# Rows scattered by half batches, the first weights spread over eight blocks, the first tiles' plan and gathers earlier, and a GpSimd drain behind the third-last tile

## The chip, the cores and the metric

One core of one Trainium2 chip. The metric is device microseconds of one execution. A run has a span, from the first to the last instruction of its record, and in every run here the time is the span plus 1.7 to 1.8 us.

A run also has a granted TensorE clock (1 is full speed) and a state, fast or slow. The state is relative to the other runs of the same kernel in the same session. That matters here: the kernel before took about 520.5 us at clock 0.99 on some chips and about 558 us at clock 0.96 on others, and both are called fast. No chip was met in both conditions, so chip and hour can't be told apart. I call the first chips undisturbed and the second disturbed, by nothing but the time of the kernel before in the same session. Runs are only compared within one session.

## The reference

Windowed attention with 8 memory keys per head, then routed experts. Sizes: 4 batches of 768 tokens, 8 heads of 64, so 512 channels; 8 experts with 1024 hidden channels; all float32.

```python
for c in range(S // 32):                       # 32 queries see 16 before, 8 after, 8 memory keys
    a = softmax(scale * q_c @ concat(mem_k, k_ctx).T)
    out[:, :, chunk] = a @ concat(mem_v, v_ctx)
x = out.transpose(0, 2, 1, 3).reshape(B, S, 512)
for b in range(B):
    prev_e = -1
    for s in range(S):
        fresh_e = argmax(logits[b, s])         # x @ w_gate
        e = fresh_e if s == 0 or local_gate[b, s] < 0.5 else prev_e
        prev_e = e
        h = relu(x[b, s] @ w1[e])
        y[b, s] = softmax(logits[b, s])[e] * (h @ w2[e])
```

## The kernel before

Attention goes in 32 blocks of 96 tokens, 8 to a batch. Routing runs beside it: logits for four blocks, the chosen expert of each token, its rank among that expert's tokens. When a whole batch is ranked, its token rows are scattered by GpSimd into a list in DRAM that is sorted by expert. The expert phase then takes tiles of 128 rows from that list. The first five tiles (the early ones) are planned from the first two batches alone, so that they can start while the other two are still being routed.

```python
def route_rows(r, b, x):                            # one whole batch
    r_ps = xps.tile([QB, NQB, E], F32, name="r_ps", tag="xps")
    for n in range(NQB):                            # NQB = 8
        nc.tensor.transpose(r_ps[:, n], rank[:, QB * n:QB * n + QB], identity=ident[:E, :E])
    # ... VectorE: rows and probabilities
    for n in range(NQB):                            # eight scatters in a row
        ins = nc.gpsimd.indirect_dma_start(out=x_dram[:, :], out_offset=..., in_=x[0:QB, n], ...)

# when what is done, in blocks
        plan_at(after, n + 3, lambda b=b, half=half: route_ranks(routes[b], b, half))
        if half:
            plan_at(after, n + 3, lambda b=b: route_places(routes[b]))
            plan_at(after, n + 4, rows, b)
    n = NQB * FORE + HALF + 5
    plan_at(after, n, plan_begun)
    plan_at(after, n + 1, planned)
    plan_at(after, NB - 5, early_gathered)          # gathers of the five early tiles
    for n in range(NB - 6, NB):
        plan_at(after, n, some_pieces, 1 if n < NB - 4 else FULL)   # weights of tiles 0 and 1
    # ... attention blocks
        if n == NB - 1:
            first_turned()                          # tile 0's rows transposed
    # ... expert phase
    for i in range(SURE):                           # 24 tiles
        ht = hidden(xt, w1_sb, between.get(i, {}))
        # ... transposes of the next tile
        stored = product(ht, w2_sb, tile_xs[i], past)   # ends with the tile's scatter
```

The order of TensorE's matmuls is fixed by the program in the attention phase and in tile 0, so one matmul that waits holds up all behind it. `xps` is a ring of two PSUM buffers that all transposes of the attention phase share.

## Time and profile before

| | time, us | granted clock |
|---|---|---|
| the run that the profile shows | 520.58 | 0.993 |
| timed runs | 559.29, 557.59, 573.73 | not listed |

The profile's own run is 39 us shorter than the median of the timed ones. One line of the page of the kernel before, beside those that the prediction shows: the granted clock in 40 slices of the span in tenths.

```profile
PEclk9999999999999999999999999999999999999997
```

No slice but the last is below nine tenths of full speed, and the profiled run itself took 520.58 us. So either the timed runs met another condition, or their 39 us more lie outside the span.

### The profile page before, as it was taken

How to read it: one execution, taken by the hardware profiler on the slowest of the kernel's cores; microseconds unless marked ns; L12 is line 12 of the kernel's file. 1: busy time of each engine (PE TensorE's matmuls, PEld its weight loads, DVE VectorE, ACT ScalarE, POOL GpSimd, SP SyncE). 2: the span in 40 equal slices, each digit the busy share in tenths (PEclk: the TensorE clock that was granted, in tenths of full speed). 3: DMA queues.
4: the chain of work that ended last, by engine and by line, in shares of the span. 5: the costliest groups of instructions: out<-in, count | busy, mean ns of one | idle time of the engine just before them, and what ended most of it. 6: DMA issues, size and time to landing. Idle time of an engine off the chain costs nothing. (4 is left out here: it accounts for less than half of the span.)

```text
span 518.9 us, 9415 instructions
## 1 busy us (share of the span) xinstructions
PE 503.4 (97%) x3606; PEld 384.5 (74%) x3606; DVE 98.0 (19%) x362; ACT 113.2 (22%) x234; POOL 96.8 (19%) x141
## 2 busy tenths in 40 slices
PE   8999999999999999999999999999999999999991
PEld 5999898876777777777777777777777777677770
DVE  1456667663330000000000000000001000000000
ACT  4555555521111111010111101111011101011110
POOL 2000323444343111001112222111211000100000
PEclk9999999999999999999999999999999999999997
DMA  9987797599999999999898899999998881299200
GB/s 301 368 258 233 199 348 224 197 392 360 406 343 390 416 415 412 419 397 354 312 330 324 327 336 358 342 340 351 358 320 327 295 317 51 87 405 415 112 21 18
DMA packets 52760, 157.97 MB, mean 304 GB/s; under 512 B 7708, under 2 KB 11806, under 8 KB 52705
## 3 DMA queue, kind: packets, MB, share of 16 engines
q1 hardware_dynamic: 44352, 135.40, 71.2%
q0 software_dynamic: 6720, 20.78, 10.8%
q10 hardware_dynamic: 1632, 1.08, 0.7%
q8 instruction: 32, 0.52, 0.4%
q14 instruction: 24, 0.19, 0.1%
HBM read 144.62 MB, written 13.40 MB: 305 GB/s over the span
## 5 line engine op out<-in xcount | busy, mean ns | idle before, releaser
L754 PE MATMUL y_ps<-w_sb,ht 128*128 128x512 f32 x416 | 183.0, 592 | 0.0
L743 PEld LDWEIGHTS h_ps<-gxt,w_sb 128*128 128x128 f32 x1408 | 160.7, 192 | 10.1 <-issue 10.0
L743 PE MATMUL h_ps<-gxt,w_sb 128*128 128x128 f32 x1408 | 161.1, 275 | 0.0
L754 PEld LDWEIGHTS y_ps<-w_sb,ht 128*128 128x128 f32 x416 | 76.9, 190 | 86.6 <-issue 85.4
L759 POOL DMA_INDIRECT out_dram<-y,to x27 | 27.2, 1006 | 228.6 <-ACT y L758 195.2
L680 DVE COPY gxt<-g_ps 128x512 f32<-128x512 f32 x22 | 15.2, 691 | 273.5 <-PE g_ps L677 273.4
L746 ACT ACTIVATE ht<-h_ps 128x512 f32<-128x512 f32 x54 | 32.3, 597 | 154.4 <-PE h_ps L743 153.0
L758 ACT ACTIVATE y<-y_ps,xs 128x512 f32<-128x512 f32 x24 | 16.5, 687 | 162.6 <-PE y_ps L754 149.8
L613 PE MATMUL o_ps<-vt,pt 128*96 128x65 f32 x512 | 49.3, 249 | 0.1
L613 PEld LDWEIGHTS o_ps<-vt,pt 128*96 128x96 f32 x512 | 46.1, 165 | 2.3 <-issue 0.6
L461 POOL DMA_INDIRECT x_dram<-x,row x32 | 30.5, 953 | 73.8 <-DVE fresh L404 63.6
L613 PEld LDWEIGHTS s_ps<-qt,kt 64*128 64x128 f32 x512 | 29.9, 188 | 6.2 <-issue 2.6
L613 PE MATMUL s_ps<-qt,kt 64*128 64x96 f32 x512 | 32.7, 277 | 0.5 <-ACT pt L344 0.4
L743 PE MATMUL h_ps<-held_xt,w_sb 128*128 128x128 f32 x256 | 29.3, 275 | 0.9 <-ACTq _compat.py:109 0.9
L743 PEld LDWEIGHTS h_ps<-held_xt,w_sb 128*128 128x128 f32 x256 | 28.9, 192 | 1.7 <-ACTq _compat.py:109 1.7
L344 ACT ACTIVATE pt<-s_ps,mask_mid 128x256 f32<-128x256 f32 x72 | 28.2, 481 | 5.8 <-PE s_ps L613 5.7
L354 DVE TENSOR_TENSOR x<-o_ps,rinvs 96x256 f32<-96x256 f32 x64 | 26.1, 417 | 1.5 <-DMA x_dram<-x,row 0.3
L362 ACT COPY xt<-xt_ps 128x384 f32<-128x384 f32 x32 | 15.3, 479 | 34.2 <-PE xt_ps L613 34.2
L572 POOL DMA_INDIRECT xs<-x_dram,rows_late x19 | 18.3, 961 | 13.2 <-DMA x_dram<-x,row 7.7
L353 DVE RECIPROCAL rinvs<-o_ps 96x4 f32<-96x4 f32 x64 | 10.5, 171 | 36.0 <-PE o_ps L613 34.2
L756 POOL TENSOR_TENSOR to<-xs,past_late 128x1 int32<-128x1 int32 x19 | 3.5, 185 | 69.2 <-DMA out_dram<-y,to 64.7
L613 PE MATMUL xt_ps<-ident,x 96*128 96x96 f32 x128 | 16.0, 247 | 0.0
(162 smaller groups left out, 209.3 us busy)
## 6 DMA issues: line engine op xcount, KB each, us to landing
w_sb<-in_w_dram SPq DMA_DIRECT2D x216, 512.0 KB, 8.1
kt<-in_k_dram SPq DMA_DIRECT2D x32, 256.0 KB, 4.5
vt<-in_v_dram SPq DMA_DIRECT2D x28, 260.0 KB, 4.4
qt<-in_q_dram SPq DMA_DIRECT2D x32, 192.0 KB, 4.0
vt<-in_v_dram ACTq DMA_DIRECT2D x4, 260.0 KB, 4.8
x_dram<-x,row POOLq DMA_INDIRECT x32, 7.9
out_dram<-y,to POOLq DMA_INDIRECT x27, 6.5
xs<-x_dram,rows_late POOLq DMA_INDIRECT x19, 6.9
```

Source lines behind the costliest of these rows:

```text
L344: nc.scalar.activation(pt[:, :, :, c], st[:, :, :, c], ACT.Exp, bias=m[:, g:g + 1], scale=SCALE)
L354: nc.vector.tensor_tensor(x[:, 0:D].rearrange("p (a u d) -> p u a d", u=2, d=DH)[:, u], o_ps[:, :, 0:DH], rinv.to_broadcast([QB, HP, DH]), ...
L362: nc.scalar.copy(xt, xt_ps)
L461: ins = nc.gpsimd.indirect_dma_start(out=x_dram[:, :], out_offset=bass.IndirectOffsetOnAxis(ap=row[:, n:n + 1], axis=0), in_=x[0:QB, n].bi ...
L572: ins = nc.gpsimd.indirect_dma_start(out=xs.bitcast(I32), out_offset=None, in_=x_dram[:, :], in_offset=bass.IndirectOffsetOnAxis(ap=rows[: ...
L613: return lambda *a, **k: tc.keep_in_program_order(f(*a, **k))
L680: nc.vector.tensor_copy(xt, g_ps)
L743: nc.tensor.matmul(h_ps[:, m], lhsT=w1_sb[:, kk, P * (g + m):P * (g + m) + P], rhs=xt[:, kk], start=(kk == 0), stop=(kk == DK - 1))
L746: nc.scalar.activation(ht[:, g:g + 4], h_ps, ACT.Relu)
L754: nc.tensor.matmul(y_ps, lhsT=ht[:, m], rhs=w2_sb[:, m], start=(m == 0), stop=(m == FK - 1))
L758: nc.scalar.activation(y, y_ps, ACT.Copy, scale=xs[:, D:D + 1])
L759: return nc.gpsimd.indirect_dma_start(out=out, out_offset=bass.IndirectOffsetOnAxis(ap=to, axis=0), in_=y, in_offset=None, bounds_check=NT ...
```

## The change

Five intents. (1) A GpSimd drain behind the third-last tile, so that the last drain finds little left. (The profile lists it on GpSimd's sequencer, as POOLq DRAIN; the last one ended 0.13 us behind the landing of GpSimd's last scatter in the ten profiles with the new drain and 5.35 to 5.84 us behind it in the ten without, as shown below.) (2) A faster start: one warm-up matmul less, q and k first and on two queues. (3) Tile 0's rows transposed two blocks earlier. (4) The plan, the early gathers and the weights of tiles 0 and 1 sooner, these in single pieces over eight blocks. (5) Rows ranked and scattered by half batches, four scatters in a row, so that the gathers can start sooner.

```diff
-WARM = 4
+WARM = 3
-    def load_qk(n):
+    def load_qk(n, queue=nc.sync):
...
+    qks = {n: load_qk(n, nc.scalar) for n in range(2)}
+    qks.update({n: load_qk(n) for n in range(2, LOADS - 2)})
+    vts = {n: load_v(n) for n in range(LOADS - 2)}
...                                              # gate loads from ScalarE's queue to SyncE's
-    def route_rows(r, b, x):
+    def route_rows(r, b, half, x):
-        for n in range(NQB):
+        for n in range(HALF):
             ins = nc.gpsimd.indirect_dma_start(
...
-        if half:
-            plan_at(after, n + 3, lambda b=b: route_places(routes[b]))
-            plan_at(after, n + 4, rows, b)
+        plan_at(after, n + 3, lambda b=b, half=half: route_places(routes[b], half))
+        plan_at(after, n + 4, rows, b, half)
...
-    n = NQB * FORE + HALF + 5
+    n = NQB * FORE + HALF + 2
     plan_at(after, n, plan_begun)
     plan_at(after, n + 1, planned)
-    plan_at(after, NB - 5, early_gathered)
-    for n in range(NB - 6, NB):
-        plan_at(after, n, some_pieces, 1 if n < NB - 4 else FULL)
+    plan_at(after, n + 2, early_gathered)
+    plan_at(after, NB - 3, first_turned)
+    for n in range(NB - 8, NB):
+        plan_at(after, n, some_pieces, 1)
...
         stored = product(ht, w2_sb, tile_xs[i], past)
+        if i == SURE - 3:
+            tc.keep_in_program_order(nc.gpsimd.drain())
```

More of the change, by code (lines that the diff above doesn't have):

```diff
@@ L45 @@
 PAIR = 2
-FULL = 2
 FAR = 4096
-WARM = 4
+WARM = 3
 QUARTER = 32
@@ L262, in load_qk, with load_v @@
         kt = ld.tile([P, HP, P], F32, name="kt")
-        nc.sync.dma_start(kt, k[n])
+        queue.dma_start(kt, k[n])
         return qt, kt
-    def load_v(n, queue):
+    def load_v(n):
         vt = ld.tile([P, H, VW], F32, name="vt")
-        queue.dma_start(vt, v[n])
+        nc.sync.dma_start(vt, v[n])
         return vt
-    qks = {n: load_qk(n) for n in range(LOADS - 2)}
-    vts = {n: load_v(n, nc.scalar) for n in range(LOADS - 2)}
+    qks = {n: load_qk(n, nc.scalar) for n in range(2)}
+    qks.update({n: load_qk(n) for n in range(2, LOADS - 2)})
+    vts = {n: load_v(n) for n in range(LOADS - 2)}
     wg = once.tile([P, DK, QUARTER], F32, name="wg")
     nc.vector.memset(wg, 0.0)
-    nc.scalar.dma_start(wg[:, :, 0:E], w_gate.rearrange("(k p) e -> p k e", p=P))
-    nc.scalar.dma_start(wg[:, :, E:E + 1], w_local.rearrange("(k p) e -> p k e", p=P))
+    nc.sync.dma_start(wg[:, :, 0:E], w_gate.rearrange("(k p) e -> p k e", p=P))
+    nc.sync.dma_start(wg[:, :, E:E + 1], w_local.rearrange("(k p) e -> p k e", p=P))
     fixed = {}
@@ L432, in route_ranks @@
         nc.vector.tensor_tensor_scan(rank[:, of_half], onehot[:, of_half], onehot[:, of_half],
-                                     rank[:, HQ - 1:HQ] if half else base[b], ALU.add, ALU.max)
-        if half:
-            nc.vector.tensor_copy(base[b + 1], rank[:, S - 1:S])
-    def route_places(r):
-        onehot, rank = r["onehot"], r["rank"]
-        for half in range(2):
-            h = slice(HQ * half, HQ * half + HQ)
-            nc.vector.tensor_tensor(rank[:, h], rank[:, h], onehot[:, h], op=ALU.mult)
-        tot = r["tot"] = sm.tile([QB, NQB, 1], F32, name="tot")
-        nc.vector.tensor_reduce(tot, r["ex"], axis=AX.X, op=ALU.add)
+                                     r["edge"] if half else base[b], ALU.add, ALU.max)
@@ new lines, in route_ranks, with route_places @@
+        if half == 0:
+            r["edge"] = sm.tile([E, 1], F32, name="edge")
+        nc.vector.tensor_copy(base[b + 1] if half else r["edge"], rank[:, HQ * half + HQ - 1:HQ * half + HQ])
+    def route_places(r, half):
+        onehot, rank = r["onehot"], r["rank"]
+        h = slice(HQ * half, HQ * half + HQ)
+        nc.vector.tensor_tensor(rank[:, h], rank[:, h], onehot[:, h], op=ALU.mult)
+        tot = r["tot"] = sm.tile([QB, HALF, 1], F32, name="tot")
+        nc.vector.tensor_reduce(tot, r["ex"][:, HALF * half:HALF * half + HALF], axis=AX.X, op=ALU.add)
@@ L445, in route_places @@
         nc.vector.tensor_scalar(tot, tot, 1e-9, None, ALU.add)
         nc.vector.reciprocal(tot, tot)
-    def route_rows(r, b, x):
-        rank, tot, ex = r["rank"], r["tot"], r["ex"]
-        r_ps = xps.tile([QB, NQB, E], F32, name="r_ps", tag="xps")
-        for n in range(NQB):
-            nc.tensor.transpose(r_ps[:, n], rank[:, QB * n:QB * n + QB], identity=ident[:E, :E])
-        row = sm.tile([QB, NQB], I32, name="row", bufs=2)
+    def route_rows(r, b, half, x):
+        j = HALF * half
+        rank, tot, ex = r["rank"], r["tot"], r["ex"][:, j:j + HALF]
+        r_ps = xps.tile([QB, HALF, E], F32, name="r_ps", tag="xps")
+        for n in range(HALF):
+            nc.tensor.transpose(r_ps[:, n], rank[:, QB * (j + n):QB * (j + n) + QB], identity=ident[:E, :E])
+        row = sm.tile([QB, HALF], I32, name="row", bufs=2)
@@ L455, in route_rows @@
         nc.vector.tensor_reduce(row, r_ps, axis=AX.X, op=ALU.max)
         nc.vector.scalar_tensor_tensor(ex, r_ps, 0.0, ex, ALU.is_gt, ALU.mult)
-        prob = sm.tile([QB, NQB, 1], F32, name="prob")
+        prob = sm.tile([QB, HALF, 1], F32, name="prob")
         nc.vector.tensor_reduce(prob, ex, axis=AX.X, op=ALU.add)
-        nc.vector.tensor_tensor(x[0:QB, :, D:D + 1], prob, tot, op=ALU.mult)
-        for n in range(NQB):
+        nc.vector.tensor_tensor(x[0:QB, j:j + HALF, D:D + 1], prob, tot, op=ALU.mult)
@@ L461, in route_rows @@
+        for n in range(HALF):
             ins = nc.gpsimd.indirect_dma_start(
                 out=x_dram[:, :], out_offset=bass.IndirectOffsetOnAxis(ap=row[:, n:n + 1], axis=0),
-                in_=x[0:QB, n].bitcast(I32), in_offset=None).ins
+                in_=x[0:QB, j + n].bitcast(I32), in_offset=None).ins
             tc.declare_no_dep(ins, group="scatters", query=mybir.DependencyQuery.ANY_SYNC, reason="rows are unique")
@@ L634, in half_turned, with rows @@
         logits_turned(lts.pop(g), routes[b]["lt"][:, HALF * half:HALF * half + HALF])
-    def rows(b):
-        route_rows(routes.pop(b), b, xs.pop(b))
+    def rows(b, half):
+        route_rows(routes[b], b, half, xs[b])
     first, after = {}, {}
@@ L652, in everything @@
         plan_at(after, n + 3, lambda b=b, half=half: route_ranks(routes[b], b, half))
-        if half:
-            plan_at(after, n + 3, lambda b=b: route_places(routes[b]))
-            plan_at(after, n + 4, rows, b)
+        plan_at(after, n + 3, lambda b=b, half=half: route_places(routes[b], half))
+        plan_at(after, n + 4, rows, b, half)
     early = {}
@@ L712, in everything @@
         if n + LOADS - 2 < NB:
-            vts[n + LOADS - 2] = load_v(n + LOADS - 2, nc.sync)
-        if n == NB - 1:
-            first_turned()
+            vts[n + LOADS - 2] = load_v(n + LOADS - 2)
         if n > 0:
@@ L779, in everything @@
     left = [f for n in range(NB, NB + HALF + 3) for f in first.pop(n, []) + after.pop(n, [])]
-    TURN, EXPERTS_0, RANKS_0, LOGITS, TURNED, PICKS, EXPERTS_1, RANKS_1, PLACES, ROWS = left
-    between = {0: {1: [TURN], 3: [LOGITS], 4: [EXPERTS_0], 5: [TURNED], 6: [RANKS_0, PICKS]},
-               1: {1: [EXPERTS_1], 2: [RANKS_1, PLACES], 7: [ROWS]}}
+    (TURN, EXPERTS_0, RANKS_0, PLACES_0, LOGITS, ROWS_0, TURNED, PICKS, EXPERTS_1, RANKS_1, PLACES_1,
+     ROWS_1) = left
+    between = {0: {1: [TURN], 3: [LOGITS], 4: [EXPERTS_0], 5: [TURNED], 6: [RANKS_0, PLACES_0, PICKS]},
+               1: {0: [ROWS_0], 1: [EXPERTS_1], 2: [RANKS_1, PLACES_1], 7: [ROWS_1]}}
     late = None
```

## The prediction

> **What bounds the kernel now.** I read the page first, then the idle time of each engine, then the timeline around the joints, last the instructions that each source line left.
>
> ```profile
> span 518.9 us, 9415 instructions
> PE 503.4 (97%) x3606; PEld 384.5 (74%) x3606; DVE 98.0 (19%) x362; ACT 113.2 (22%) x234; POOL 96.8 (19%) x141
> PE   8999999999999999999999999999999999999991
> ```
>
> TensorE is busy for 503.4 of 518.9 us, so 15.5 us is all that a change which only moves work can win, unless it also removes matmuls. Only the first and last of the 40 slices are below nine tenths. So I looked up what the idle 15.5 us are: first the waits of TensorE.
>
> ```profile
> PE z_ps L256 <- DVE xs L253: 1.6, 1, 1.6
> PE h_ps L743 <- ACTq _compat.py:109: 0.9, 1, 0.9
> PE h_ps L613 <- DVE held_xt L680: 0.7, 1, 0.7
> PE s_ps L613 <- ACT pt L344: 0.4, 1, 0.4
> PE s_ps_early L613 <- ACT xt L362: 0.2, 1, 0.2
> ```
>
> That is 3.8 us (columns: total, times, longest), a few gaps of 0.1 us more. The 0.7 us is tile 0's first product waiting for its turned rows, the 0.9 us is the branch for the optional tiles. From tile 3 on the second products start exactly 14.45 us apart but at the branch comparisons, so no weights, gathers or scatters hold TensorE there. The rest, 10.9 us, is the tail: TensorE ends at about 508.0 us. What fills it is in the sequencer's instructions of the kernel's last line:
>
> ```profile
> L856 SPq EVENT_SEMAPHORE  x14: 17/28/27574, 484.7 to 518.8; - x14
> L856 POOLq DRAIN  x3: 40/113/7862, 510.2 to 518.6; - x3
> L759 POOL DMA_INDIRECT out_dram<-y,to x27: 971/1011/1020, 130.6 to 509.5; - x27
> ```
>
> (min/median/max in ns, first and last start in us.) The last row scatter starts at 509.5. SyncE's wait of 27.57 us from 484.7 ends at 512.3: that is its landing. But GpSimd's drain, begun at 510.2, takes 7.86 us, to 518.0, and the closing barrier (0.8 us) stands behind it. So 518.0 - 512.3 = 5.7 us at the end wait for GpSimd's drain alone. The page's chain of waits does not show this, because a drain is a sequencer's instruction and not counted as work.
>
> [...] Here the warm-up passes start 0.85 us apart up to the one at 5.98, then 0.73 and 0.43: warm some 5 us after the first. [...]
>
> **The change, part by part.**
>
> 1. **Drain behind the third-last tile.** The program issues 1 plain and 32 + 27 + 19 + 7 + 5 = 90 indirect DMAs on GpSimd before the end; 7862 ns / 91 = 86 ns each, if the drain goes through all of them. For that reading: the drains with nothing (more) to settle are short (0.19 us at the start, 0.11 and 0.04 us after the long one), so it is no fixed price. The new drain sits where GpSimd is idle: that tile's scatter starts at 481.0, the next at 495.5. 89 x 86 ns = 7.7 us fit into the 14.5. Two scatters remain for the last drain: 0.2 us by the estimate, so it should be done when the last scatter has landed, 512.3. SyncE is ready for the barrier at 513.1 as it is now, and the barrier's 0.75 us follow: end at 513.8 in place of 518.8. **-5.0 us.**
>
> 2. **One warm-up matmul less.** It is two passes, those at 6.71 and 7.14; the first scores start at 7.67. They now start when the sixth pass lets go, at about 6.71, if their data is there. It was: q0 landed at 3.95, k0 at 5.68, with four v loads (260 KB each) sharing the way. These v loads now go behind the q and k loads, and q0 and k0 leave on two queues at once, so both come earlier. The gate loads leave ScalarE's queue, so its table load (6.35 now) is no new obstacle. The following wait of 0.41 us for the first exponentials moves with it. v0 is wanted at about 11.4; being the ninth load, it lands by 8 to 10. **-0.96 us.**
>
> 3. **Turned rows of tile 0 two blocks earlier.** Its wait of 0.73 us before the first product goes: **-0.7 us.** The price: its PSUM goes into the same two-buffer ring as the routing's, behind c_ps, which VectorE's 1.0 us scan still reads, and VectorE's copy (0.69 us) stands behind that half's ranks. I take **+0.5 us** for the two.
>
> 4. **Plan three blocks earlier.** The two sums' matmuls only move; their wait of 0.22 us behind ACT's copy should go, as l_ps no longer stands in the same block: **-0.2 us.** SyncE waited 7.9 us for the plan's table before the first weight piece; the weights now start some 9 us earlier. That buys nothing on TensorE, which waits for no weights now.
>
> 5. **Rows by halves.** VectorE, TensorE and GpSimd do the same sizes in twice the pieces (8 more small VectorE instructions a batch, 0.15 to 0.2 us each, on an engine about 70% busy in this phase; not on the path). On the path is the ring of two PSUM buffers. In the two timeline lines of a block with logits alone, and the three of a block with rows too:
>
> ```profile
> 43.60 0.50 PE L613 MATMUL xt_ps<-ident,x 96*128 96x96 f32 x4
> 43.93 0.60 PE L613 MATMUL l_ps<-ident,lt_sb 128*96 128x128 f32 x4
> ...
> 56.25 0.50 PE L613 MATMUL xt_ps<-ident,x 96*128 96x96 f32 x4
> 56.68 0.54 PE L613 MATMUL r_ps<-ident,rank 8*96 8x8 f32 x8
> 57.32 0.64 PE L613 MATMUL l_ps<-ident,lt_sb 128*96 128x128 f32 x4
> ```
>
> Without r_ps, l_ps takes the buffer of the logits and starts 0.33 us after xt_ps. With r_ps between, it takes xt_ps's own buffer and must wait for ACT to copy that out: 1.07 us after. The eight transposes filled that wait almost; four won't, but the release time stays. So blocks 14, 22 and 30 stay as they are, and blocks 10, 18 and 26, which get an r_ps now, lose 1.07 - 0.33 = 0.74 each: **+2.2 us.** The last batch's rows lie between tile 0's and 1's products, where there is no such ring pressure: 0.
>
> Sum: -5.0 - 0.96 - 0.7 + 0.5 - 0.2 + 2.2 = **-4.2 us**, 0.8% of 559.3. The timed runs lie about 40 us above the span; I take differences over one to one. 559.3 - 4.2 = **555.0 us**.
>
> **Rivals.** (a) The last drain doesn't get shorter: its length is a price of the last scatter's landing, or it goes through every DMA of the execution again. For it: it ends 5.7 us after the landing, and only one drain behind DMAs was measured. Then parts 2 to 5 alone count, +0.8 us: 560. I give it 1 in 5. (b) Tile 0's gather becomes TensorE's bound. It needs all scatters of two batches landed (about 94 us) and took 8.0 us to land under weight traffic, so it lands at 102 to 104; the transposes in block 29 want it at about 104.5. Against it: only four scatters stand before it instead of eight. The order of matmuls is pinned, so a late gather stops everything: up to +2 us, 557. (c) The PSUM ring costs nothing, for ACT's copy may be out of the way sooner: then -6.4 us, 553. (d) More weights beside q, k and v starve the attention blocks: q, k and v are 708 KB a block of 3.1 us, 228 GB/s, and a 512 KB piece adds 165, together below the 416 GB/s that the trace reaches; unlikely.
>
> **Range and chances.** Eight in ten: 551 to 559.5. Below are (c) and a faster run; above are (a) and (b) together, or a median that falls on a slow run (one of three took 573.7). For 2% the change would have to win 11.2 us, more than tail and attention waits together allow without fewer matmuls: 0.03. Slower by 2% would need a stall of 15 us: 0.02. Within 2%: 0.95.
>
> **What would show it.** Part 1: a GpSimd drain of some 7 to 8 us from about 482 less the shift, the last one under 3 us, the span's end about 5.8 us behind the last matmul's end (10.9 now). Part 2: first scores at about 6.7. Part 3: no wait before tile 0's first product. Part 5: l_ps about 1.1 us behind xt_ps in blocks 10, 18 and 26, and the attention phase (first scores to tile 0's first product, 104.3 us now) 1 to 2 us longer. Wrong if the last drain still takes 6 us or more, if TensorE waits for the gather, or if tile 0's first product starts more than 1.5 us away from its 111.95.

## The result, and the profile after

| | before | after |
|---|---|---|
| runs, us | 559.29, 557.59, 573.73 (slow), 559.62 | 542.31, 543.01, 540.04, 550.19 (slow) |
| median, us | 559.45 | 542.66 |
| granted clock of the runs | not listed | 0.972, 0.968, 0.980, 0.951 |

The ratio is 0.9695 (95% interval 0.9641 to 0.9749): faster by 3.0%, where 0.8% was predicted. Here and below a ratio is the mean time of one kernel's fast runs over that of the other's of the same rounds, so not quite the ratio of the medians that I quote.

The page of the kernel after:

```profile
span 540.6 us, 9452 instructions
...
PE   8997897889899999999999999999999999999995
...
PEclk9999989956999999999999999999999999999998
```

This span is 21.7 us *longer* than the one in the profile of before, in a kernel that is faster. So the two profiles are of different conditions, and laying one over the other explains nothing. TensorE now has idle time in the slices of the attention phase, and in the slices 9 and 10 its clock is near half (5 and 6 tenths). TensorE's waits in the same run (total, times, longest):

```profile
PE o_ps L615 <- issue: 6.2, 12, 1.0
PE lt_ps L615 <- DVE onehot L423: 2.0, 2, 1.0
PE lt_ps L615 <- ACT xt L363: 2.0, 1, 2.0
PE l_ps L615 <- ACT xt L363: 1.6, 6, 0.3
```

Three of these have no counterpart before: before, the waits with a name came to 3.8 us and none stood at o_ps. Only the fourth was predicted (the PSUM ring). The drains, from the sequencer's instructions (min/median/max ns, first and last start):

```profile
L860 POOLq DRAIN  x3: 46/112/2561, 536.6 to 540.3; - x3
...
L820 POOLq DRAIN  x1: 8550/8550/8550, 507.2 to 507.2; - x1
```

The long drain of 7.86 us at the end is now one of 8.55 us where GpSimd is idle, and 2.56 us remain at the end. That part is as predicted; 12 us of gain are not.

### The profile page after: what moved, and what is told of

It reads as the page before. It is cut to its first block, busy times and chain, and to the rows that moved or that the text cites. A ratio compares the mean times of both kernels' runs of the same rounds, so it can differ in the third digit from the quotient of the medians.

```text
span 540.6 us, 9452 instructions
## 1 busy us (share of the span) xinstructions
PE 517.5 (96%) x3604; PEld 395.8 (73%) x3604; DVE 103.0 (19%) x394; ACT 112.5 (21%) x234; POOL 95.8 (18%) x141
## 5 line engine op out<-in xcount | busy, mean ns | idle before, releaser
L759 POOL DMA_INDIRECT out_dram<-y,to x27 | 27.3, 1010 | 235.6 <-ACT y L758 192.3
L615 PE MATMUL o_ps<-vt,pt 128*96 128x65 f32 x512 | 57.2, 268 | 6.3 <-issue 6.2
L615 PEld LDWEIGHTS o_ps<-vt,pt 128*96 128x96 f32 x512 | 53.3, 183 | 10.7 <-issue 8.0
L615 PEld LDWEIGHTS s_ps<-qt,kt 64*128 64x128 f32 x512 | 31.5, 196 | 6.6 <-issue 4.6
L615 PE MATMUL s_ps<-qt,kt 64*128 64x96 f32 x512 | 34.6, 286 | 0.6 <-ACT pt L345 0.4
L363 ACT COPY xt<-xt_ps 128x384 f32<-128x384 f32 x32 | 15.4, 482 | 42.1 <-PE xt_ps L615 32.4
L615 PE MATMUL xt_ps<-ident,x 96*128 96x96 f32 x128 | 18.2, 270 | 0.5 <-ACT xt L363 0.5
```

Of the source, the lines that this page charges most:

```text
L363: nc.scalar.copy(xt, xt_ps)
L615: return lambda *a, **k: tc.keep_in_program_order(f(*a, **k))
L759: return nc.gpsimd.indirect_dma_start(out=out, out_offset=bass.IndirectOffsetOnAxis(ap=to, axis=0), in_=y, in_offset=None, bounds_check=NT ...
```

## The experiments

All 18 runs gave the right result. Two theories came up on the way, S with e5 and G with e8:

- **Theory G**: the gain beyond the sum comes from the earlier gathers. In the kernel before tile 0's gather lands less than 1 us ahead of its use; under disturbance it comes late and holds up TensorE.
- **Theory S**: the gain comes from shorter rows of scatters. On a disturbed chip TensorE is held up while GpSimd issues a row of scatters, and four in a row hold it up less than eight.

### The sum, on one chip: both kernels and the drain alone

Four kernels in one session: the two as they are, before with the drain alone, after without it.

**e1_before**: no edit.

> The kernel before, unchanged, to see what its timed executions (557 to 574 us) look like, since its profiled execution took only 520.6 us at a granted clock of 0.993. Theory A (the lost clock): a usual execution shows a span of about 556 us, a mean granted clock of 0.93 to 0.96, stretches at half clock in the attention phase (first 140 us) and gaps on TensorE there; the expert phase and the 10.9 us tail are as in the profile seen. Rival B (the time lies outside the span): spans stay near 519 us at 0.99 and the time is 40 us longer. Ratio to itself 1.00.

**e2_after**: no edit.

> The kernel after, unchanged, in the same rounds. Ratio 0.97 if the result was no matter of chip or hour. Theory A: its executions spread as their granted clock does, roughly 540 us at 0.97, 549 at 0.95, and one with no half-clock stretch would take about 514 us. Rival B: no such relation.

**e3_before_drain**: before, with

```diff
         stored = product(ht, w2_sb, tile_xs[i], past)
+        if i == SURE - 3:
+            tc.keep_in_program_order(nc.gpsimd.drain())
```

> The kernel before with the one drain behind the third-last tile alone. Tail theory: the last drain falls from 7.9 to under 3 us, the stretch from the last matmul to the end from 10.9 to about 6, time -5 us, ratio 0.991. Rival: the drain accounts for all of the change (ratio 0.97), or for nothing (1.00).

**e4_after_nodrain**: after, without these two lines.

> The kernel after without its drain. Tail theory: tail back to 10.9 us, time 5 us above the kernel after, ratio to before about 0.979, so the other 12 us come from the other parts. Rival: without the drain nothing of the gain is left (1.00).

| chip 12 | median, us | ratio to before (95%) | tail, us |
|---|---|---|---|
| e1_before | 520.68 | 1.0001 (0.9988 to 1.0015) | 10.88 |
| e2_after | 515.87 | 0.9910 (0.9897 to 0.9924) | 5.92 |
| e3_before_drain | 515.89 | 0.9906 (0.9891 to 0.9921) | 6.15 |
| e4_after_nodrain | 521.11 | 1.0007 (0.9994 to 1.0021) | 10.88 |

(The tail is the span from the end of the last matmul to the end. One run of e3 was slow, 530.36 us at clock 0.97, and is left out.)

On this chip the kernel before takes 520.5 us, and the change is worth 4.6 us, where the prediction's sum says 4.2. All of it is the drain: alone it gives the same as the whole change, and the change without it gives nothing. So the prediction's arithmetic was right *for this chip*, and the 3.0% of the result belong to another condition. The predicted ring wait is in the trace of e2_after, in a block that got an r_ps, on TensorE's timeline (start, duration, in brackets the idle time before and what ended it):

```profile
41.62 0.50 PE L615 MATMUL xt_ps<-ident,x 96*128 96x96 f32 x4
42.05 0.35 PE L615 MATMUL r_ps<-ident,rank 8*96 8x8 f32 x4
42.68 0.64 PE L615 MATMUL l_ps<-ident,lt_sb 128*96 128x128 f32 x4 [0.29 <-ACT xt L363]
```

l_ps starts 1.06 us behind xt_ps; 1.07 was predicted.

### Halves without the early plan, and the early plan without halves

**e5_after_full_rows**: after, with the rows again ranked and scattered by whole batches.

```diff
-        plan_at(after, n + 3, lambda b=b, half=half: route_places(routes[b], half))
-        plan_at(after, n + 4, rows, b, half)
+        if half:
+            plan_at(after, n + 3, lambda b=b: route_places(routes[b]))
+            plan_at(after, n + 4, rows, b)
# and the bodies of route_ranks, route_places and route_rows as before
```

> The kernel after with its rows scattered by whole batches again (eight scatters in a row in place of two times four); all else as after. On an undisturbed chip (before at 520.5, after at 515.9): the ring theory of the prediction says the halves cost 0.74 us in each of three blocks, so this is 2.2 us faster than after, some 513.7, ratio to before 0.987. On a disturbed chip, as the first pair's (before 558, after 542): theory S (TensorE's semaphores get stuck behind a long row of scatters, and the idle clock then falls to half) says this kernel loses most of the gain there, ratio 0.985 to 0.995, with longer gaps at the end of each row of eight. Rival C (the disturbance strikes by chance, no matter what the scatters do): ratio 0.97 as the kernel after.

**e6_before_half_rows**: before, with the same lines the other way round: half batches, all else as before.

> The kernel before with its rows scattered by half batches and nothing else of the change. Undisturbed: ring theory: 2.2 us slower than before, ratio 1.004. Disturbed: theory S: most of the gain beyond the tail's 5 us, 558 to about 546 to 548, ratio 0.98. Rival C: ratio 1.00 on either.

**e7_after_again**: after, no edit, to have it on the same chip.

> The kernel after again, as the yardstick of this call's chip. Undisturbed: ratio 0.991 as before. Disturbed: ratio 0.97. If the executions of before in the same rounds lie at 520.5 with a granted clock of 0.993, the chip is undisturbed, and the first pair's gain of 3% can't be looked into here.

| chip 6 | median, us | ratio to before (95%) |
|---|---|---|
| e5_after_full_rows | 523.47 | 1.0038 (1.0010 to 1.0067) |
| e6_before_half_rows | 531.22 | 1.0201 (1.0188 to 1.0215) |
| e7_after_again | 515.82 | 0.9903 (0.9888 to 0.9917) |

This chip was undisturbed too, so theory S was not tested here, and both expectations missed (e5 at 513.7 us, e6 0.4% above before). TensorE's timeline at tile 0's transposed rows in e5_after_full_rows:

```profile
108.53 1.08 PE L614 MATMUL g_ps<-ident,xs 128*128 128x128 f32 x4 [5.29 <-DMA xs<-x_dram,rows_early]
```

and in e6_before_half_rows:

```profile
119.08 1.09 PE L614 MATMUL g_ps<-ident,xs 128*128 128x128 f32 x4 [6.61 <-DMA xs<-x_dram,rows_early]
```

Either half of the idea alone makes the gather late. In e5 the gather is early in program order, but it must wait for eight scatters in a row: the last one landed at 100.19, the gather was issued at 100.98 and landed at 108.39. In e6 the scatters are early, but the first four scatters of batch 2 now stand ahead of the late gather on GpSimd, which issues it at 111.84, after the last of the four has landed at 110.96. And the idle time is not all: a stretch at half clock comes with it. The view of stretches (bounds, length, busy time with counts for PE, PEld, DVE, ACT, POOL, then the granted clock, the DMA share and GB/s) has it, in e5:

```profile
106.90:120.50 13.60, 11.97 (x71) 10.16 (x72) 5.54 (x27) 1.66 (x4) 1.29 (x6) 0.50 0.95 366
```

and in e6:

```profile
114.50:124.70 10.20, 5.48 (x26) 5.21 (x27) 3.00 (x16) 0.71 (x2) 7.20 (x11) 0.50 1.03 403
```

So parts 4 and 5 need each other, and rival (b) of the prediction, a late gather, is real; the change as made stays clear of it.

### Theory G, on a disturbed chip

The gathers are made late by chains of tiny GpSimd copies of the row numbers ahead of them (21 copies; the gathers read the last copy). By G, before then loses 6 to 10 us, and after, whose gather has 4 to 5 us to spare, next to nothing.

**e8_before_late**: before, with

```diff
     def early_gathered():
+        table, rows, past = early["tiles"]
+        a, c = slow                       # two small tiles
+        nc.gpsimd.tensor_copy(a, rows)
+        for _ in range(20):
+            nc.gpsimd.tensor_copy(c, a)
+            a, c = c, a
+        early["tiles"] = table, a, past
         early["xs"] = [gathered(early["tiles"], i, range(FORE)) for i in range(EARLY)]
```

> The kernel before with the first tiles' gathers made later by a chain of 21 tiny copies on GpSimd (some 4 us by 0.19 us each). In the kernel before tile 0's gather lands 0.7 to 0.9 us before TensorE wants it. Theory G (the slack of this gather is what the change buys): TensorE stands idle some 3 us before the turned rows of tile 0, [...]and the time grows by 6 to 10 us (ratio 1.012 to 1.02). Rival: the idle costs itself alone, +3 us (1.006), with no half clock.

**e9_after_late**: after, with the same lines.

> The kernel after with the same chain. There the gather lands some 4 to 5 us before it is wanted. Theory G: no idle stretch, or one under 1 us, and a time within 1 us of the kernel after (ratio 0.991 to before). The pair's ratio then grows from 0.99 to about 0.975 by the same disturbance, as on the first chip. Rival: it loses as much as the kernel before does.

**e10_after_old_start**: after, with part 2 undone.

```diff
-WARM = 3
+WARM = 4
# and q, k, v and gate loads on the queues of before
```

> The kernel after with four warm-up matmuls and the old queues for the first loads (part 2 undone). The prediction's term: +0.96 us against after (516.8 if after is 515.9). First scores at about 7.7 us. Rival, since the granted clock rises at another moment in each execution (4.5 to 7.6 us after the start so far): nothing that stands out of the spread, 0 to 0.5.

**e11_before_look**: before, no edit, to have its profile on the same chip as the others.

> The kernel before once more, to see its trace should this call's chip be disturbed as that of the first pair (executions of 557 us in place of 520.5). If so, theory G expects an idle stretch of several us before tile 0's turned rows and long stretches at half clock around it; theory S expects stops of TensorE at the ends of the rows of scatters. If the executions are at 520.5, it tells nothing new.

| chip 7 | median, us | ratio to before (95%) |
|---|---|---|
| before, 11 runs | 558.22 | |
| e8_before_late | 560.05 | 1.0055 (0.9993 to 1.0117) |
| e9_after_late | 544.91 | 0.9736 (0.9665 to 0.9807) |
| e10_after_old_start | 543.51 | 0.9682 (0.9627 to 0.9738) |
| e11_before_look | 561.39 | 1.0050 (0.9962 to 1.0139) |

(The medians are of all runs. One run each of before, e8 and e9 and two of e10 were slow; the ratios leave them out.)

This chip was disturbed: before takes 558 us at clocks of 0.947 to 0.960 in its fast runs. So this condition is one of some chips in some sessions, and the pair of the result had it. Theory G falls. The copies did delay the gather in before, on TensorE's timeline in e8_before_late:

```profile
136.66 1.08 PE L613 MATMUL g_ps<-ident,xs 128*128 128x128 f32 x4 [4.26 <-DMA xs<-x_dram,slow]
```

Yet e8 lost 0.55%, not shown to differ from nothing, where G expected 1.2 to 2%. And with the gather as it was, in the trace of e11_before_look, TensorE doesn't wait at g_ps at all. (e9 speaks neither for nor against G: its trace has no wait at g_ps, as G expected too.) Part 2 is no part of the 12 us either: without it after is as fast as in the result.

What e11_before_look has instead, on the timeline of GpSimd and TensorE, is this:

```profile
61.20 1.57 PE L613 MATMUL o_ps<-vt,pt 128*96 128x65 f32 x16
61.46 0.92 POOL L461 DMA_INDIRECT x_dram<-x,row  x1 [0.30 <-issue]
...
62.69 0.92 POOL L461 DMA_INDIRECT x_dram<-x,row  x1 [0.30 <-issue]
62.86 0.38 PEld L613 LDWEIGHTS c_ps<-ident,pick 96*40 96x40 f32 x4
62.94 0.53 PE L613 MATMUL c_ps<-ident,pick 96*40 96x96 f32 x4
...
67.58 0.92 POOL L461 DMA_INDIRECT x_dram<-x,row  x1 [0.30 <-issue]
...
71.01 2.79 PE L613 MATMUL o_ps<-vt,pt 128*96 128x65 f32 x16 [7.54 <-remote]
```

A row of eight scatters runs from 58.94 to 68.5. After the fourth, TensorE stops for 7.54 us. "Remote" means that a semaphore's update ended the wait for which the record has no instruction. What TensorE waits for is that others read what it has made, and these get to know of it late. ScalarE's timeline in the same run:

```profile
70.43 0.48 ACT L362 COPY xt<-xt_ps 128x384 f32<-128x384 f32 x1 [3.17 <-remote]
```

It copies out transposes that TensorE had ended at 63.11 (62.61 + 0.50), and ScalarE was free from 67.3 on (66.06 + 1.20, its instruction before). In e1_before the same copy, on ScalarE's timeline:

```profile
63.50 0.48 ACT L362 COPY xt<-xt_ps 128x384 f32<-128x384 f32 x1 [0.36 <-PE xt_ps L613]
```

Here the transposes ended at 63.46, so the news took 0.04 us; on the disturbed chip 7.3 us. VectorE too stands 9.82 us until 70.28 for a product of TensorE that ended at 62.77. The kept trace also holds the semaphores' updates, which `prof` does not list. The semaphore that TensorE raises has, after 61.68, its next updates at 65.98, 70.26, 70.35, 70.41 and 70.47, and SyncE, ScalarE and VectorE each start 0.01 to 0.02 us behind one of them. So these engines were not late for want of their own instructions; the updates came late. The same place on GpSimd's and TensorE's timeline in e1_before, on an undisturbed chip:

```profile
63.30 0.49 PE L613 MATMUL c_ps<-ident,pick 96*40 96x96 f32 x4
63.63 1.50 PE L613 MATMUL o_ps<-vt,pt 128*96 128x65 f32 x16
64.26 0.92 POOL L461 DMA_INDIRECT x_dram<-x,row  x1 [0.30 <-issue]
64.96 0.50 PE L613 MATMUL xt_ps<-ident,x 96*128 96x96 f32 x4
```

The same scatters at the same distances, and TensorE goes on. The stops repeat at each row: in e11_before_look 5.07 us at 102.8 with batch 1's, 1.28 and 1.38 us about the five gathers, 2.93 us at 149.5 with batch 2's; batch 3's has only 1.2 us in three gaps. With each of these but batch 3's comes a stretch at half clock. The view of stretches in e11_before_look:

```profile
58.00:74.00 16.00, 8.46 (x91) 7.98 (x90) 4.60 (x23) 3.96 (x10) 7.62 (x9) 0.79 0.76 217
...
101.00:115.00 14.00, 7.95 (x54) 5.99 (x56) 3.88 (x10) 3.26 (x8) 3.06 (x4) 0.51 0.36 103
```

and in e1_before:

```profile
58.00:74.00 16.00, 15.96 (x212) 14.74 (x210) 10.33 (x47) 8.76 (x23) 7.75 (x8) 1.00 0.94 272
```

In the profile of after, also of a disturbed chip, a row of four scatters looks so:

```profile
60.06 0.92 POOL L463 DMA_INDIRECT x_dram<-x,row  x1 [11.31 <-DVE x L461]
...
63.53 0.47 PE L615 MATMUL o_ps<-vt,pt 128*96 128x65 f32 x3
63.74 0.92 POOL L463 DMA_INDIRECT x_dram<-x,row  x1 [0.30 <-issue]
64.35 0.29 PE L615 MATMUL o_ps<-vt,pt 128*96 128x65 f32 x1 [0.35 <-issue]
65.06 0.22 PE L615 MATMUL o_ps<-vt,pt 128*96 128x65 f32 x1 [0.42 <-issue]
65.77 1.74 PE L615 MATMUL o_ps<-vt,pt 128*96 128x65 f32 x11 [0.50 <-issue]
```

The row ends about where the long stop began in e11: 1.27 us in three gaps. These short gaps are not of the same kind. Two of the three stand before instructions that wait for no semaphore, so late updates do not explain them. Theory S speaks of both, but not of how they arise. It needed a test of its own, as after differs from before in much else.

### Theory S: a pause in the row, nothing else

**e12_before_pause**: before, with a chain of 29 tiny GpSimd copies (some 7.8 us) between the fourth and the fifth scatter, in batches 0 and 2 only. The work is the same and GpSimd has more of it; nothing comes earlier. By S this is faster on a disturbed chip and the same on an undisturbed one.

```diff
         for n in range(NQB):
+            if n == HALF and b % 2 == 0:
+                a, c = slow
+                nc.gpsimd.tensor_copy(a, row)
+                for _ in range(28):
+                    nc.gpsimd.tensor_copy(c, a)
+                    a, c = c, a
+                row = a
             ins = nc.gpsimd.indirect_dma_start(
```

> The kernel before with one thing added: in batches 0 and 2 a chain of 29 tiny copies on GpSimd (some 7.8 us) stands between the fourth and the fifth scatter, so that a row of eight becomes two of four; batches 1 and 3, the plan, the gathers and TensorE's program are as before. Theory S (on a disturbed chip TensorE's semaphore updates are held up from about the fourth scatter of a row until the row has been worked off): on a disturbed chip (before at 557) the long stops near 63 and 147 us shrink from 3 to 7.5 us to about 2, with less half clock: -5 to -9 us, ratio 0.984 to 0.991. On an undisturbed chip (before at 520.5): no change, ratio 0.999 to 1.001. Rival C (the stops come by chance or from the load in general): 1.00 on both.

**e13_after_full_rows_2**: the kernel of e5 again, meant for a disturbed chip.

> The kernel after with rows scattered by whole batches, as in an earlier run, in the hope of a disturbed chip. Theory S: there stops of 3 to 7 us return at the ends of the rows of eight, the time is 9 to 13 us above the kernel after (542 to 543), ratio to before 0.985 to 0.995. Rival C: 0.97 there. On an undisturbed chip: 523.5 again (1.0038), from the late gather and 13.65 us at half clock after it.

The chip (14) was undisturbed: e12 520.82 us, 1.0004 (0.9991 to 1.0017); e13 521.20 us, 1.0030 (1.0003 to 1.0058), with a gap of 4.95 us at tile 0's gather, as in e5. That is S's answer for an undisturbed chip, but it doesn't tell S from no effect at all.

**e14_before_pause_2**, the same kernel:

> The pause in the row of scatters again, for want of a disturbed chip in the last call. Disturbed chip (before at 557): theory S: -5 to -9 us, ratio 0.984 to 0.991, the stops near 63 and 147 us down to about 2 us each. Rival C: 1.00. Undisturbed chip: 1.000 again, which tells nothing new.

Chip 11, undisturbed: 520.76 us, 1.0002 (0.9987 to 1.0016).

**e15_before_pause_3**, the same kernel:

> As the last run: on a disturbed chip (before at 557), theory S: -5 to -9 us, ratio 0.984 to 0.991; rival C: 1.00. Undisturbed: 1.000, nothing new.

Chip 6, undisturbed: 520.84 us, 1.0008 (0.9994 to 1.0022).

**e16_before_pause_4**, the same kernel:

> As before: on a disturbed chip (before at 557), theory S: -5 to -9 us, ratio 0.984 to 0.991; rival C: 1.00. Undisturbed: 1.000, nothing new.

Chip 2, disturbed: before 558.45 us. With the pause the fast runs were 553.79, 547.32, 550.41 and 547.23 us, two more were slow (561.96 and 557.61). Ratio of fast runs **0.9842 (0.9799 to 0.9885)**: 8.8 us less for *more* work on GpSimd. That shows S for two of the batches' rows. (Slow means over 1.5% above a kernel's own fastest run, which leaves out 557.61 here, where before's fast runs lie. Over all runs the medians are 552.10 and 558.45, still 6.4 us apart.) The interval reaches across 2%, so as a verdict of its own size it is unclear, but it lies wholly below 1.

The profile fell on a slow run, so its times are not compared, only the places of its stops: 2.93 us in one place beside batch 0's two rows of four; 5.9 us in eight gaps beside batch 1's eight, which had no pause; 0.3 us beside batch 2's two rows of four; besides 2.4 us about the gathers and 1.4 us in three gaps behind batch 3's eight. The first of these and three of the eight, on TensorE's timeline:

```profile
81.12 2.80 PE L621 MATMUL o_ps<-vt,pt 128*96 128x65 f32 x16 [2.93 <-remote]
...
111.34 0.37 PE L621 MATMUL o_ps<-vt,pt 128*96 128x65 f32 x2 [0.89 <-issue]
...
112.77 0.33 PE L621 MATMUL xt_ps<-ident,x 96*128 96x96 f32 x2 [0.89 <-issue]
114.18 0.32 PE L621 MATMUL c_ps<-ident,pick 96*40 96x96 f32 x1 [1.08 <-issue]
```

So a pause helps but is no cure: even four scatters may hold TensorE up for 2.93 us. And rows of scatters are not all of it: this slow run was at half clock from 11.67 to 42.39 us, before any scatter, with no gap of TensorE over 1.1 us until then.

### A version to beat both: rows one block later

The PSUM ring costs after 2 us on any chip. If the rows come one block later, r_ps no longer stands in a block with l_ps.

**e17_after_rows_later**: after, with

```diff
-        plan_at(after, n + 4, rows, b, half)
+        plan_at(after, n + 5, rows, b, half)
# and the list of what is left behind the last block in the new order
```

> The kernel after with each half's row transposes one block later, where no logits stand between them and the block's other PSUM uses. Ring theory (the wait of 1.07 us from xt_ps to l_ps is a price of r_ps standing between them): l_ps starts 0.33 us after xt_ps again in six blocks, r_ps costs 0.32 us one block on: 0.42 us a half won, six halves: -2.5 us against after, 513.4 on an undisturbed chip (ratio to before 0.986). The scatters and gathers come 3 us later, which eats most of the 4 to 5 us of the gather's slack. Rival: that slack is not enough, TensorE waits for the gather, half clock follows, 520 or more.

**e18_after_rows_later_2**: the same kernel, for the other kind of chip.

> The kernel after with each half's row transposes one block later, again, as the last call's chip was disturbed. Undisturbed chip: ring theory: -2.5 us against after, 513.4 (ratio to before 0.986), l_ps 0.33 us behind xt_ps. Rival: the gathers, 3 us later, come too late, a stop before tile 0's turned rows and half clock: 518 or more. Disturbed chip: about 0.983 as in the last call.

| | chip | median, us | ratio to before (95%) |
|---|---|---|---|
| e17_after_rows_later | 2, disturbed | 548.86 | 0.9831 (0.9796 to 0.9867) |
| e18_after_rows_later_2 | 6, undisturbed | 515.49 | 0.9881 (0.9865 to 0.9896) |

On the undisturbed chip the ring wait goes (from the first scores to block 28's transposes 96.69 us, where e2_after has 98.83), but tile 0's gather comes a block later too: in the profiled run TensorE stands 2.31 us at g_ps and then runs 10.24 us at half clock. That run took 520.33 us, the others 513.38 to 515.78. On the disturbed chip the trace has a stretch of 37.55 us at half clock from 89.61 on, and the ratio is worse than the 0.9695 of after, though from another session. So on an undisturbed chip it is level with after or slightly ahead (0.988, where e2 and e7 have 0.991 and 0.990 in other sessions), and on a disturbed one it is behind; after stays the safer of the two.

## Why the prediction was wrong

**The step that failed** is "The timed runs lie about 40 us above the span; I take differences over one to one." There is no overhead of 40 us. Time is span plus 1.7 to 1.8 us in every run, also in that profile (520.58 against 518.9). The profile was of an undisturbed run, the timed ones were of a disturbed chip, whose span is 556 us (so judged by their level, as their clocks are not listed). The 37 us between them are stops and half clock in the attention phase and the start of the expert phase, which the profile of before couldn't show. From the traces of before:

| | e1_before, undisturbed | e11_before_look, disturbed | after, disturbed |
|---|---|---|---|
| span, us | 518.9 | 555.7 | 540.6 |
| TensorE idle before its last matmul (from 2 us on), us | 3.4 | 25.6 | 15.4 |
| half clock before the tail, us | 0 | 37.5 | 27.3 |
| of this with TensorE at work, some us | 0 | 26 | 27 |
| tail, us | 10.88 | 10.87 | 6.20 |

Half clock costs about half of the time at work in it, by my estimate from the profile of after: 32 matmuls of s_ps took 2.03 us at full clock (from 38.31) and 3.73 us at half (from 117.67). So the disturbed run of before is 22.2 + 26/2 = 35 us longer than the undisturbed one; measured 36.8. And from e11_before_look to after it is 10.2 us less idle and 4.7 us less tail, 14.9 of 15.1 us, with the half clock at work unchanged. Predicted was the tail alone, within 0.8 us. The prediction's own sign of being wrong, tile 0's first product more than 1.5 us away from 111.95, shows the two conditions too: it starts at 135.50 in the profile of after and at 111.22 in e2_after.

**The step that failed with it** is part 5's "GpSimd do the same sizes in twice the pieces", judged by the PSUM ring alone, and the list of rivals, which had no stop from a row of scatters in it. The 10 us of idle time went where rows of eight became rows of four. That rows hold up TensorE on a disturbed chip is shown by e16 against e12, e14 and e15, and by the traces. (e16's own profile is of a slow run, so it can't show that the stops were shorter in the fast ones.) That the halves account for all of after's 10 us is argued from the places of the stops only: after with whole rows (e13) never met a disturbed chip.

The other points, by the prediction's own steps:

1. *Drain, -5.0 us*: right. Tail 10.88 to 5.92 (e2_after) and 6.15 (e3_before_drain); times -4.6 us for the drain alone. Its sizes were off without harm. In the ten profiles that have it, the drain in mid phase took 8.43 to 8.79 us, not 7.7, and the last one 2.28 to 2.78 us, not 0.2. So 86 ns for each DMA does not hold for few. In all ten the last one ends 0.13 us behind the last update of the last scatter's landing (in the result's profile 539.15 and 539.02), whatever its length: it waits for that landing, and SyncE's wait of 27.39 us, behind which the barrier comes, ends there too, at 539.04 in the result's profile. In the ten profiles without the new drain the last one goes on for 5.35 to 5.84 us behind the landing, so that part comes from the drain and not from the landing, as the prediction read it. Rival (a) is refuted.
2. *Start, -0.96 us*: right in the mean, but small against its own scatter. First scores stood at 6.75 to 8.23 us in the eleven profiles with the old start (mean 7.39) and at 5.76 to 6.97 us in the nine with the new one (mean 6.48), 0.91 us earlier.
3. *Tile 0's rows earlier, -0.7 us*: right. The wait of 0.73 us at h_ps is gone. In e2_after tile 0's gather landed at 100.07, 5.2 us ahead of its use at 105.23; before it was 0.7 us ahead.
4. *Plan earlier, -0.2 us*: no gain of its own on an undisturbed chip, but needed: with halves alone (e6) before loses 2.0%.
5. *Ring, +2.2 us*: right; 1.9 us (first scores to block 28's transposes 96.95 us before, 98.83 in e2_after). Rival (c) is refuted.

Parts 2 to 5 together, +0.8 us by the prediction, are +0.6 us by the medians (e4_after_nodrain), and the whole is -4.6 us against -4.2, all on undisturbed chips. The chance of 0.03 for over 2% was argued from "more than tail and attention waits together allow", with the waits read from the one undisturbed profile. (A slip without effect: 559.3 less the sum is 555.1 us, not 555.0.)

**What stays open**: what makes a chip disturbed (chips 2 and 7 and that of the result were, 6, 11, 12 and 14 were not; chip 6 in three sessions); why semaphore updates come late behind a row of scatters there; why TensorE also stands, for up to 1.3 us at a time, where it waits for nothing that the profile shows; why half clock can come before any scatter (e16); and why the longest stop after eight varies from under 1 to 7.5 us.

## What to carry to other kernels

Before you use a profile, check that its span is that of the timed runs; a difference is not overhead until it is shown to be, and a "fast" run is fast only beside its own session. Judge a long row of GpSimd DMAs also by what it may do to the other engines: break it up, since in the disturbed traces here eight in a row stopped TensorE for up to 7.5 us at a time and four for up to 2.9, and half clock came with most of the long stops. Move the drain of many GpSimd DMAs to a place where GpSimd is idle; it gave 4.6 of 520 us on the one chip where it was tried alone, and all ten profiles with it have a tail of 5.9 to 6.2 us in place of 10.9.

## What the traces show of drains, semaphore updates and the clock

- A GpSimd drain took 0.19 us with nothing to settle (at 0.39 in the profiles of before and after), 7.85 to 8.17 us behind 91 DMAs (7.86 in the profile of before), 8.43 to 8.79 us behind 89 (8.55 in that of after), and 2.28 to 2.78 us for the two after those (2.56). SyncE's EVENT_SEMAPHORE of 27.57 us in the profile of before covers a wait, and ends with the landing of the last scatter at 512.3.
- With eight scatters in a row on a disturbed chip, in e11_before_look, TensorE stood 7.54 and 5.07 us for semaphore updates, and 2.93 us for a copy by ScalarE. The same kernel on an undisturbed chip, in e1_before, had none of these waits.
- The same kernel has two levels by the chip or the session it meets, 520.5 and 558 us on one core, both called fast beside their own runs.
- Half clock before the tail lasted 6.83 and 20.48 us in the profile of after, 13.65 us in e5_after_full_rows, 10.24 us in e18_after_rows_later_2, 30.72 us in e16_before_pause_4 and 37.55 us in e17_after_rows_later. It went on while TensorE worked: in e5_after_full_rows TensorE worked again from 108.53 and the clock stayed at half until 120.5, and in the profile of after it stayed at half for 20.48 us from 110.49, with TensorE busy for 20.33 of them. There TensorE had been idle for some 2 us in the 6 us before, in gaps of 0.64 us at most.
